# Top-32 attention with two expert layers: scores copied to SBUF by ScalarE, PSUM banks moved from scores to experts

## The chip, the core and the metric

One core of one Trainium2 chip runs the whole program. The metric is device time in microseconds of one execution. The kernel before was timed three times, and its median is 1330.06 us (1329.61 to 1332.45).

The engines are named as the profile names them: PE is TensorE's matmul side and PEld its weight loads, DVE is VectorE, ACT is ScalarE, POOL is GpSimd, and SP issues the DMAs. SBUF is the large on-chip memory, PSUM the small one (eight banks) that PE writes.

## The reference, cut to what matters

```python
# q, k, v: (4, 8, 576, 64)
scores = matmul(q, k^T) / 8
kth    = the 32nd largest score of each row
scores = where(scores >= kth, scores, -1e9)
attn   = exp(scores - rowmax);  attn /= attn.sum() + 1e-9
x      = matmul(attn, v)                       # -> (2304 tokens, 512)
h      = x @ w_in                              # 512 -> 2048
g      = where(h >= 1, h, where(h <= -1, 0, (h + 1)**2 / 4))
x      = g @ moe_w_out                         # 2048 -> 512
y      = silu(x @ w_gate) * (x @ w_val)        # 512 -> 1536
out    = y @ moe2_w_out                        # 1536 -> 512
```

All of it is in float32. The kernel gets there with TensorE's float32r format: nearly each operand is split into a high and a low part, and an expert product takes three passes.

## The kernel before, in words

The attention is worked in 32 units, a pair of heads by two or three query tiles of 128 rows. There are 144 score tiles of 128 queries by 576 keys. For each one PE writes scores into one of two PSUM tiles `pS` (two banks each), and DVE finds the 32nd largest value there: MAX8 (eight largest of a row, line 686) and MATCH_REPLACE8 (strike them out, line 696) take turns, the first of each reading `pS` and the later ones a copy `R` in SBUF that the first strike has written. ACT reads `pS` too and writes the exponentials into `E` (line 693). Last, DVE's mask (line 700, a scalar_tensor_tensor) compares `pS` with the 32nd value, multiplies with `E`, and sums the row. It holds `pS` until then, so PE's next score into this tile waits for it. The 576 entries of a row of `E` are then transposed on PE through two banks `pT`, moved out by ACT (lines 723 to 734), split on POOL (line 736), and multiplied with `v`.

The experts run between and behind, through two banks `pM`: first products on line 967, the second product of the first layer on 1009, that of the second layer on 1081. Their results are worked on by ACT and DVE (lines 1043 to 1115) and split by ACT and POOL (lines 873 and 875). All of the 68 weight slabs (512 KB) are split once on the chip, "converted" (lines 827 to 850): three operations on ACT, two on POOL, and on DVE one scalar_tensor_tensor (line 832), which reads one operand from `pM` in the first 24 slabs and both from SBUF in the other 44. The converted slab is stored to DRAM and loaded again for each step.

Nothing of the order is written by hand. A planner (`Plan`) gives each operation a cost by formulas, runs a list schedule forward and backward a few times over all engines and buffer rings, and emits the instructions of each engine in the order it finds. Each engine then executes its own queue in order, with semaphore waits. So a changed cost or ring size moves instructions on all engines.

Of the kernel before, what the change touches and what calls it, by code (L numbers as in the profile page):

```python
# [331 lines left out]
class Kernel:  # L332
# [53 lines left out]
    def dma(self, out, in_, nbytes, reads=(), writes=(), prio=5, tag="dma"):  # L386
        nc = self.nc
        self.p.op("DMA", nbytes / Plan.DMA_RATE, lambda: nc.sync.dma_start(out=out(), in_=in_()),
                  reads, writes, prio, tag, lat=Plan.DMA_LAT)


    def build(self):
# [9 lines left out]
        self.r_E = R("E", [128, 2, S], F32, 3)  # L402
# [118 lines left out]
    def prep_q(self, b, hp, qts):  # L521
# [80 lines left out]
    def outputs(self, b, hp, blk, V, PT, rs, rc):  # L602
# [7 lines left out]
        for h in (0, 1):  # L610
# [9 lines left out]
            p.op("ACT", self.act(N), lambda a=a, z=z, av=av: nc.scalar.activation(  # L620
# [33 lines left out]
    def qtile(self, t, i, qT, qz, kT, rs):  # L654
# [5 lines left out]
        for h in (0, 1) if t < 4 else (0,):  # L660
# [32 lines left out]
            p.op("ACT", self.act(576, self.FN - self.SB), lambda h=h, sc=sc, ee=ee: nc.scalar.activation(  # L693
                out=ee(), in_=sc(), func=AF.Exp, bias=nb[:, h:h + 1], scale=0.125), [ps, (nb, h)], [(Eb, h)], 1, "exp")
            for k in range(3):
                p.op("DVE", self.dve(576) + 0.06 + (0 if k else self.PS), lambda h=h, k=k, sc=sc, rr=rr: nc.vector.match_replace(  # L696
# [540 lines left out]
```

## Time and profile before

| what | value |
|---|---|
| timed runs, median (lowest to highest) | 1330.06 us (1329.61 to 1332.45) |
| profiled execution, span from first to last instruction | 1326.2 us |
| median less span (what lies around it) | 3.9 us |
| busy in the span: PE / DVE / ACT / POOL | 1208.5 / 1017.7 / 876.4 / 778.3 us |
| of the chain that ended last: PE / DMA / ACT / DVE / POOL | 68 / 9 / 7 / 7 / 6 % |
| matmuls | 7832 |

Busy time is the union of an engine's instructions. The profiled execution has no time of its own beside its span; the timed runs are other executions, and their median stands 3.9 us over it. The chain follows back from the last instruction to what released it, again and again. Shares over the whole span mix stages of different kind, so the rows further down are cut by stretches of time.

### The profile page before, as it was taken

To read this page: it belongs to the slowest core of one execution; us is meant where nothing else is said; L and a number is where in the kernel's file an instruction comes from. 1 tells how busy PE (TensorE), PEld (TensorE's weight loads), DVE (VectorE), ACT (ScalarE), POOL (GpSimd) and SP (SyncE) were. 2 spreads that over 40 slices of the span, in tenths; PEclk is the share of its full clock that TensorE was granted. 3 is DMA by queue.
4 is the path that set the end of the run, shared out by engine and by line. 5 is a ranking of instruction groups with operands and counts; after the bars stand their busy time and mean duration, and the time that the engine had idled before them with its cause. 6 is when DMAs were issued, how large, how long until landed. Compare 5 with 4: busy or idle time off the path is not lost.

```text
span 1326.2 us, 23321 instructions
## 1 busy us (share of the span) xinstructions
PE 1208.5 (91%) x7832; PEld 1095.6 (83%) x7832; DVE 1017.7 (77%) x2066; ACT 876.4 (66%) x1926; POOL 778.3 (59%) x831
## 2 busy tenths in 40 slices
PE   2556589888899999999999999999999999999998
PEld 2444489886799989998999988889999888888887
DVE  5899999899899989999999898989999312212212
ACT  6889799889777578776879777767766322333220
POOL 7888868689856465866667665556655313213210
PEclk9666699999899999999999999999999999999999
DMA  8788879789877786778676854548666754666452
GB/s 279 276 287 272 287 262 350 280 269 337 294 272 280 276 320 240 297 263 304 232 275 227 318 196 128 176 162 288 216 252 249 283 198 146 248 220 220 163 191 64
DMA packets 137032, 328.18 MB, mean 247 GB/s; under 512 B 21072, under 2 KB 66640, under 8 KB 136912
## 3 DMA queue, kind: packets, MB, share of 16 engines
q1 hardware_dynamic: 136912, 326.68, 70.2%
q8 instruction: 62, 1.02, 0.3%
q14 instruction: 58, 0.48, 0.1%
HBM read 282.07 MB, written 44.56 MB: 246 GB/s over the span
## 4 chain that ended last, share of the span: by engine, by line
PE 68%; DMA 9%; ACT 7%; DVE 7%; POOL 6%; issue 3%; SPq 0%; DVEq 0%; POOLq 0%; ACTq 0%
PE pM L967 25%; PE pM L1009 10%; PE pM L1081 7%; PE late L967 7%; PE pS L672 4%; PE pT L615 4%; PE late L1081 3%; PE pT L747 3%; DVE v L686 2%; PE late L1009 2%; DVE R L696 2%; POOL ct L835 2%; DMA cv<-in_moe_w_val_dram 2%; DMA cv<-in_moe_w_out_dram 1%; DMA w<-ws_moe_w_out 1%
## 5 line engine op out<-in xcount | busy, mean ns | idle before, releaser
L686 DVE MAX8 v<-R 128x8 f32<-128x576 f32 x432 | 315.1, 749 | 0.8
L967 PE MATMUL pM<-w,w 128*128 128x256 f32 (+1 forms) x1719 | 295.8, 319 | 3.5 <-DVE t L1105 2.5
L967 PEld LDWEIGHTS pM<-w,w 128*128 128x128 f32 x1719 | 249.9, 196 | 19.7 <-DVE t L1105 2.6
L736 POOL TENSOR_TENSOR PT<-F,PT 128x384 fp32r<-128x384 f32 (+2 forms) x192 | 176.7, 930 | 90.8 <-ACT F L734 84.4
L875 POOL TENSOR_TENSOR w<-t,w 128x512 fp32r<-128x512 f32 x110 | 142.2, 1295 | 135.1 <-ACT w L873 113.8
L696 DVE MATCH_REPLACE8 R<-v,R 128x576 f32<-128x576 f32 x288 | 213.8, 743 | 0.0
L686 DVE MAX8 v<-pS 128x8 f32<-128x576 f32 x144 | 109.3, 759 | 38.8 <-PE pS L672 36.3
L1009 PE MATMUL pM<-w,w 128*128 128x256 f32 (+1 forms) x867 | 132.2, 291 | 1.3 <-DVE t L1047 1.3
L693 ACT ACTIVATE E<-pS,nb 128x576 f32<-128x576 f32 x144 | 107.4, 746 | 25.3 <-DVE R L696 19.2
L747 PE MATMUL pT<-idf,E 128*128 128x128 f32 x512 | 95.9, 293 | 28.9 <-ACT qT L537 16.0
L1009 PEld LDWEIGHTS pM<-w,w 128*128 128x128 f32 x867 | 114.2, 190 | 4.0 <-DVE t L1047 2.7
L672 PE MATMUL pS<-kT,qT 128*128 128x288 f32 x512 | 100.9, 321 | 17.2 <-DVE E L700 14.9
L700 DVE SCALAR_TENSOR_TENSOR E<-pS,v,E 128x576 f32<-128x576 f32 x144 | 115.8, 804 | 0.2
L732 ACT ACTIVATE PT<-pT 128x384 fp32r<-128x384 f32 (+2 forms) x192 | 88.4, 463 | 40.6 <-PE pT L747 21.6
L696 DVE MATCH_REPLACE8 R<-v,pS 128x576 f32<-128x576 f32 x144 | 107.7, 748 | 0.0
L873 ACT ACTIVATE w<-t 128x512 fp32r<-128x512 f32 x110 | 70.5, 642 | 54.0 <-DVE t L1115 43.0
L835 POOL TENSOR_TENSOR ct<-ct,cv 128x512 int32<-128x512 int32 x68 | 91.4, 1348 | 22.9 <-ACT ct L830 15.1
L875 POOL TENSOR_TENSOR late<-t,late 128x512 fp32r<-128x512 f32 x32 | 41.3, 1293 | 103.8 <-ACT late L873 84.1
L747 PEld LDWEIGHTS pT<-idf,E 128*128 128x128 f32 x512 | 65.3, 148 | 42.6 <-ACT qT L537 18.1
L672 PEld LDWEIGHTS pS<-kT,qT 128*128 128x128 f32 x512 | 82.1, 206 | 22.3 <-DVE E L700 17.6
L967 PE MATMUL pM<-late,w 128*128 128x256 f32 (+1 forms) x597 | 98.5, 302 | 0.7 <-DVE t L1047 0.6
L615 PE MATMUL pT<-PT,v 128*128 128x256 f32 (+1 forms) x512 | 94.1, 310 | 3.9 <-ACT PT L727 3.1
(138 smaller groups left out, 2679.7 us busy)
## 6 DMA issues: line engine op xcount, KB each, us to landing
w<-ws_moe_w_out SPq DMA_DIRECT2D x134, 512.0 KB, 6.3
w<-ws_moe_w_in SPq DMA_DIRECT2D x90, 512.0 KB, 5.7
w<-ws_moe_w_val SPq DMA_DIRECT2D x55, 512.0 KB, 5.4
w<-ws_moe_w_gate SPq DMA_DIRECT2D x51, 512.0 KB, 6.3
late<-ws_moe_w_out SPq DMA_DIRECT2D x50, 512.0 KB, 5.3
cv<-in_moe_w_out_dram SPq DMA_DIRECT2D x28, 512.0 KB, 5.1
late<-ws_moe_w_in SPq DMA_DIRECT2D x28, 512.0 KB, 5.8
cv<-in_moe_w_in_dram SPq DMA_DIRECT2D x16, 512.0 KB, 5.0
```

Source lines behind the costliest of these rows:

```text
L615: nc.tensor.matmul(av[:, 0:N], V[:, h, c, :], PT[:, s, h * 4 + c, 0:N], start=s == 0 and c == 0, stop=False)
L672: nc.tensor.matmul(ps[:, j, 0:288], l(), kT[:, hh, at + j * 288:at + (j + 1) * 288], start=k == 0, stop=k == len(lhs) - 1)
L686: p.op("DVE", self.dve(576) + (0 if k else self.PS), lambda: nc.vector.max(out=v8[:, h, k, :], in_=rr() if k else sc()), [Rb if k else ps] ...
L696: p.op("DVE", self.dve(576) + 0.06 + (0 if k else self.PS), lambda h=h, k=k, sc=sc, rr=rr: nc.vector.match_replace(out=rr(), in_to_replace ...
L700: p.op("DVE", self.dve(576) + 0.06 + self.PS, lambda h=h, sc=sc, ee=ee: nc.vector.scalar_tensor_tensor(out=ee(), in0=sc(), scalar=v8[:, h, ...
L736: p.op("POOL", self.pool(n), lambda: nc.gpsimd.tensor_tensor(out=dst(1), in0=src(F), in1=dst(0).bitcast(F32), op=OP.subtract), [F, (PT, (0 ...
L747: fn = (lambda ps=ps, m=m, h=h, c=c: nc.tensor.transpose(ps[:, m * 128:(m + 1) * 128], Sb[:, h, 64 * h + c * 128:64 * h + (c + 1) * 128], ...
L835: p.op("POOL", self.pool(512), lambda: nc.gpsimd.tensor_tensor(out=ci(), in0=ci(), in1=word(0), op=OP.add), [(cv, 0)], [ct], 3, tag + "cvadd")
L875: p.op("POOL", self.pool(n), lambda: nc.gpsimd.tensor_tensor(out=dst[:, 1, to:to + n], in0=src[:, off:off + n], in1=dst[:, 0, to:to + n].b ...
L967: nc.tensor.matmul(ps[:, at:at + n], W[:, w, k * 128:(k + 1) * 128], x[:, s, xat:xat + n], start=k == 0 and j == 0, stop=k == KC - 1 and j ...
L1009: nc.tensor.matmul(ps[:, at:at + n], WO[f][:, v, j * 128:(j + 1) * 128], g[:, s, gat:gat + n], start=q == 0 and m == 0, stop=q == 3 and m ...
L1081: nc.tensor.matmul(ps[:], a[:, s, at:at + 128], WO[f][:, v, :], start=q == 0 and m == 0, stop=q == 3 and m == 2)
```

## The change

Each score tile is copied by ACT from PSUM into a new SBUF tile `C` (two of them), and the MAX8, the exponential, the first MATCH_REPLACE8 and the mask read `C`. With this `pS` is free once the copy is done. One `pS` tile (two banks) stays in place of two, and `pM` has four banks in place of two. `E` goes from three tiles to two. Some costs in the planner are raised: the DMA latency from 1.7 to 2.0 us, the loads of column-wise weight slabs, POOL's cost per element, two conversion operations on ACT, and ACT operations that move data between partition halves. The extra cost that the planner put on DVE operations for reading PSUM is gone from the score tile's operations, since they read SBUF now.

```diff
 class Plan:
-    DMA_LAT = 1.7
+    DMA_LAT = 2.0
...
     SB, FN, PS, PORT = 0.043, 0.136, 0.065, 0.0
+    CVX, XP = 0.045, 0.125
...
-        return 0.149 + n * 0.0021
+        return 0.149 + n * 0.00215
...
-        self.p.op("DMA", nbytes / Plan.DMA_RATE, lambda: nc.sync.dma_start(out=out(), in_=in_()),
+        rate = 310e3 if tag.endswith("ldw64") and narrow else Plan.DMA_RATE
+        self.p.op("DMA", nbytes / rate, lambda: nc.sync.dma_start(out=out(), in_=in_()),
...
-        self.r_E = R("E", [128, 2, S], F32, 3)
+        self.r_E = R("E", [128, 2, S], F32, 2)
...
-        self.p_s = R("pS", [128, 2, 512], F32, 2, "P")
+        self.p_s = R("pS", [128, 2, 512], F32, 1, "P")
+        self.r_C = R("C", [128, S], F32, 2)
-        self.p_m = R("pM", [128, 512], F32, 4 - self.PT_BANKS, "P")
+        self.p_m = R("pM", [128, 512], F32, 6 - self.PT_BANKS, "P")
...
-            def vmax(k, h=h, ps=ps, Rb=Rb, sc=sc, rr=rr):
-                p.op("DVE", self.dve(576) + (0 if k else self.PS), lambda: nc.vector.max(
-                    out=v8[:, h, k, :], in_=rr() if k else sc()), [Rb if k else ps], [(v8, (h, k))], 6, "max8")
+            Cb = self.r_C.new()
+
+            def cc(Cb=Cb):
+                return Cb[:].rearrange("p (j n) -> p j n", j=2)
+            p.op("ACT", self.act(576), lambda sc=sc, cc=cc: nc.scalar.activation(out=cc(), in_=sc(), func=AF.Copy), [ps], [Cb], 1, "scp")
+            def vmax(k, h=h, Cb=Cb, Rb=Rb, cc=cc, rr=rr):
+                p.op("DVE", self.dve(576), lambda: nc.vector.max(
+                    out=v8[:, h, k, :], in_=rr() if k else cc()), [Rb if k else Cb], [(v8, (h, k))], 6, "max8")
...
-            p.op("ACT", self.act(576, self.FN - self.SB), lambda h=h, sc=sc, ee=ee: nc.scalar.activation(
-                out=ee(), in_=sc(), func=AF.Exp, bias=nb[:, h:h + 1], scale=0.125), [ps, (nb, h)], [(Eb, h)], 1, "exp")
+            p.op("ACT", self.act(576, self.FN), lambda h=h, cc=cc, ee=ee: nc.scalar.activation(
+                out=ee(), in_=cc(), func=AF.Exp, bias=nb[:, h:h + 1], scale=0.125), [Cb, (nb, h)], [(Eb, h)], 1, "exp")
...
-            p.op("DVE", self.dve(576) + 0.06 + self.PS, lambda h=h, sc=sc, ee=ee: nc.vector.scalar_tensor_tensor(
-                out=ee(), in0=sc(), scalar=v8[:, h, 3, 7:8], in1=ee(),
+            p.op("DVE", self.dve(576) + 0.06, lambda h=h, cc=cc, ee=ee: nc.vector.scalar_tensor_tensor(
+                out=ee(), in0=cc(), scalar=v8[:, h, 3, 7:8], in1=ee(),
                 op0=OP.is_ge, op1=OP.mult, accum_out=rs[:, i, h:h + 1]),
-                [ps, (v8, (h, 3))], [(Eb, h), (rs, (i, h))], 5, "mask")
+                [Cb, (v8, (h, 3))], [(Eb, h), (rs, (i, h))], 5, "mask")
...
-        p.op("ACT", self.act(512, self.SB), lambda: nc.scalar.activation(
+        p.op("ACT", self.act(512, self.SB + self.CVX), lambda: nc.scalar.activation(
             out=bits(), in_=cv[:].bitcast(U16).rearrange("p (n t) -> p n t", t=4)[:, :, 1], func=AF.Copy,
```

The changed program has 144 instructions more, all on ACT; the count of every other instruction is the same. Three places show what moves. In these rows a name is a tile with its buffer number, and lines of the changed kernel are 3 to 8 higher (mask 700 is 708, exponential 693 is 701, copy 692, score 672 is 675).

On DVE, near the 60th score tile, before (masks on line 700 read `pS`):

```order
L700 SCALAR_TENSOR_TENSOR E_199,rs_210<-pS_250,v_204,E_199 128x576
L696 MATCH_REPLACE R_200<-v_204,R_200 128x576
L686 MAX v_204<-R_200 128x8
L696 MATCH_REPLACE R_200<-v_204,R_200 128x576
L686 MAX v_202<-pS_250 128x8
```

The same place in the changed kernel (the mask is on line 708):

```order
L708 SCALAR_TENSOR_TENSOR E_197,rs_209<-C_250,v_203,E_197 128x576
L694 MAX v_203<-R_199 128x8
L704 MATCH_REPLACE R_199<-v_203,R_199 128x576
L694 MAX v_203<-R_199 128x8
L694 MAX v_201<-C_250 128x8
```

In both, three instructions of the other tile stand between a mask and the next MAX8 that reads the same buffer. Before, PE's score has to be made in this gap; now ACT's copy has to be.

On PE, about the same place, before, with the waits (`pS1` is a score tile, `pM` an expert bank):

```order
L747 MATMUL pT0_251<-idf_160,E0_197 128x128 [waits Activation_49]
L672 MATMUL pS1_250<-kT0_193,qT0_191 128x288 [waits DVE_49]
L672 MATMUL pS1_250<-kT0_193,qT0_191 128x288 x3
L747 MATMUL pT0_251<-idf_160,E0_197 128x128 x2
L747 MATMUL pT1_252<-idf_160,E0_197 128x128 [waits Activation_49]
```

And in the changed kernel:

```order
L975 MATMUL pM3_256<-w4_224,w2_222 128x256 [waits DMAHW1_49]
L975 MATMUL pM3_256<-w4_224,w2_222 128x256 x5
L675 MATMUL pS0_248<-kT0_193,qT0_191 128x288 [waits Activation_49]
L675 MATMUL pS0_248<-kT0_193,qT0_191 128x288 x3
L975 MATMUL pM3_256<-w0_220,w2_222 128x256 x6
```

A score's wait for DVE's mask has become a wait for ACT's copy, and expert products now use banks up to `pM3`. Counted over the whole order, 239,616 columns of expert products stood ahead of PE's 201st score matmul (of 640) before, and 254,208 do now; ahead of the 161st it was 168,960 and is 179,712.

On ACT of the changed kernel, about the same place (the copies are on line 692; before, a row like them stood nowhere):

```order
L692 ACTIVATE C_249<-pS_248 128x576
L623 ACTIVATE tmp_217<-pT_252 64x320
L540 ACTIVATE qT_191<-pT_252 128x2x256
L626 ACTIVATE y_218<-pT_251 64x320
L701 ACTIVATE E_197<-C_249,nb_204 128x576
L540 ACTIVATE qT_191<-pT_252 64x2x256
L881 ACTIVATE w_231<-t_240 128x512
L540 ACTIVATE qT_191<-pT_252 64x2x256
L895 ACTIVATE t_237<-pM_253 128x512
L692 ACTIVATE C_250<-pS_248 128x576
```

What stood behind the exponential alone now stands behind a copy as well: moves out of `pT`, splits and expert results. A copy waits for PE's score and for DVE's mask of the tile two before, whose `C` it takes.

## Rows read from the trace of the kernel before

**Rows 1.** The page: span, and busy tenths of each engine in 40 slices.

```profile
span 1326.2 us, 23321 instructions
...
PE   2556589888899999999999999999999999999998
DVE  5899999899899989999999898989999312212212
ACT  6889799889777578776879777767766322333220
POOL 7888868689856465866667665556655313213210
```

**Rows 2.** Busy time by stretch (columns in the first line of the view).

```profile
core 0: us, PE busy (x) PEld busy (x) DVE busy (x) ACT busy (x) POOL busy (x), PEclk, DMA share, GB/s
0.00:100.00 100.00, 46.65 (x196) 36.63 (x196) 76.68 (x158) 80.51 (x165) 79.20 (x83) 0.75 0.82 281
100.00:200.00 100.00, 69.19 (x396) 58.71 (x397) 94.08 (x183) 88.73 (x191) 78.71 (x76) 0.76 0.79 274
200.00:300.00 100.00, 91.57 (x701) 88.73 (x700) 95.85 (x190) 85.20 (x188) 80.20 (x77) 0.97 0.86 300
300.00:400.00 100.00, 87.37 (x617) 79.80 (x616) 91.52 (x189) 82.35 (x182) 80.07 (x83) 0.97 0.85 299
...
900.00:1000.00 100.00, 97.28 (x783) 94.93 (x782) 97.05 (x205) 74.46 (x160) 57.64 (x73) 1.00 0.71 254
1000.00:1100.00 100.00, 100.00 (x593) 89.11 (x592) 45.85 (x89) 37.38 (x77) 32.81 (x35) 1.00 0.68 246
...
```

**Rows 3.** The same view, in three long stretches (same columns).

```profile
0.00:400.00 400.00, 294.77 (x1906) 263.87 (x1907) 358.13 (x717) 336.79 (x723) 318.19 (x317) 0.86 0.83 289
400.00:1040.00 640.00, 631.73 (x4676) 598.24 (x4675) 596.29 (x1258) 467.33 (x1082) 395.74 (x463) 1.00 0.71 251
1040.00:1326.00 286.00, 281.99 (x1254) 233.48 (x1252) 63.32 (x92) 72.25 (x122) 64.35 (x52) 1.00 0.53 183
```

**Rows 4.** DVE's groups of the whole span: busy us, mean ns, idle before.

```profile
L686 DVE MAX8 v<-R 128x8 f32<-128x576 f32 x432 | 315.1, 749 | 0.8
L686 DVE MAX8 v<-pS 128x8 f32<-128x576 f32 x144 | 109.3, 759 | 38.8 <-PE pS L672 36.3 <-PE pT L747 1.4 <-PE pT L544 0.5
L696 DVE MATCH_REPLACE8 R<-v,R 128x576 f32<-128x576 f32 x288 | 213.8, 743 | 0.0
L696 DVE MATCH_REPLACE8 R<-v,pS 128x576 f32<-128x576 f32 x144 | 107.7, 748 | 0.0
L832 DVE SCALAR_TENSOR_TENSOR cv<-cv 128x512 int32<-128x512 int32 x44 | 43.1, 980 | 4.5 <-ACT cv L827 3.0 <-issue 1.4
L832 DVE SCALAR_TENSOR_TENSOR cv<-cv,pM 128x512 int32<-128x512 int32 x24 | 16.5, 685 | 22.0 <-ACT pM L827 21.1 <-issue 0.9
```

**Rows 5.** Line 832: each operand pair's shortest, median and longest ns.

```profile
engine op xcount: duration ns min/median/max, first and last start us, forms
...
L832 DVE SCALAR_TENSOR_TENSOR cv<-cv x44: 669/822/1798, 102.1 to 319.3; 128x512 int32<-128x512 int32 x44
L832 DVE SCALAR_TENSOR_TENSOR cv<-cv,pM x24: 671/688/697, 7.1 to 95.4; 128x512 int32<-128x512 int32 x24
```

**Rows 6.** DVE in order of time: start us, us.

```profile
283.94 1.80 DVE L832 SCALAR_TENSOR_TENSOR cv<-cv 128x512 int32<-128x512 int32 x1
285.66 0.08 DVE L696 MATCH_VALUE_LOAD R<-v,R 128x8 f32 x1
285.73 0.74 DVE L696 MATCH_REPLACE8 R<-v,R 128x576 f32<-128x576 f32 x1
```

**Rows 7.** POOL in the same stretch.

```profile
283.87 1.32 POOL L875 TENSOR_TENSOR w<-t,w 128x512 fp32r<-128x512 f32 x1
285.12 1.80 POOL L835 TENSOR_TENSOR ct<-ct,cv 128x512 int32<-128x512 int32 x1
```

**Rows 8.** DVE's mask group from 0 to 400 us.

```profile
L700 DVE SCALAR_TENSOR_TENSOR E<-pS,v,E 128x576 f32<-128x576 f32 x49 | 39.4, 804 | 0.2
```

**Rows 9.** DVE's mask group from 400 to 1040 us.

```profile
L700 DVE SCALAR_TENSOR_TENSOR E<-pS,v,E 128x576 f32<-128x576 f32 x95 | 76.4, 805 | 0.0
```

**Rows 10.** ACT's groups of the whole span.

```profile
L693 ACT ACTIVATE E<-pS,nb 128x576 f32<-128x576 f32 x144 | 107.4, 746 | 25.3 <-DVE R L696 19.2 <-POOL nb L690 3.0 <-POOL PT L736 1.7
L501 ACT ACTIVATE kT<-pT 128x512 fp32r<-128x512 f32 x32 | 19.1, 596 | 4.5 <-PE pT L498 4.2
L883 ACT ACTIVATE big<-pM 128x512 f32<-128x512 f32 x30 | 18.1, 602 | 17.7 <-PE pM L1081 13.9 <-PE pM L1009 3.7
L873 ACT ACTIVATE w<-t 128x512 fp32r<-128x512 f32 x110 | 70.5, 642 | 54.0 <-DVE t L1115 43.0 <-DMA t<-xs 6.3 <-PE late L1081 2.7
```

**Rows 11.** POOL's groups of the whole span.

```profile
L736 POOL TENSOR_TENSOR PT<-F,PT 128x384 fp32r<-128x384 f32 x144 | 145.5, 1019 | 79.3 <-ACT F L734 75.1 <-PE pS L672 3.6 <-DMA w<-ws_moe_w_out 0.3
L875 POOL TENSOR_TENSOR w<-t,w 128x512 fp32r<-128x512 f32 x110 | 142.2, 1295 | 135.1 <-ACT w L873 113.8 <-PE pM L1009 11.8 <-issue 6.2
L835 POOL TENSOR_TENSOR ct<-ct,cv 128x512 int32<-128x512 int32 x68 | 91.4, 1348 | 22.9 <-ACT ct L830 15.1 <-DVE cv L832 3.0 <-DMA cv<-in_moe_w_val_dram 1.6
```

**Rows 12.** Waits from 0 to 400 us: total us, times, longest.

```profile
PE pS L672 <- DVE E L700: 14.1, 9, 5.8
DVE v L686 <- PE pS L672: 5.9, 9, 1.8
```

**Rows 13.** Waits from 400 to 1040 us.

```profile
DVE v L686 <- PE pS L672: 30.4, 48, 1.6
```

**Rows 14.** The chain that ended last: one piece in order of time.

```profile
1042.61 27.90 PE pM L967 x123
```

More of the change, by code (lines that the diff above doesn't have):

```diff
@@ L384, in mm, with dma @@
         return k * (0.0133 + n / 2400.0)
-    def dma(self, out, in_, nbytes, reads=(), writes=(), prio=5, tag="dma"):
+    def dma(self, out, in_, nbytes, reads=(), writes=(), prio=5, tag="dma", narrow=False):
         nc = self.nc
-        self.p.op("DMA", nbytes / Plan.DMA_RATE, lambda: nc.sync.dma_start(out=out(), in_=in_()),
+        rate = 310e3 if tag.endswith("ldw64") and narrow else Plan.DMA_RATE
+        self.p.op("DMA", nbytes / rate, lambda: nc.sync.dma_start(out=out(), in_=in_()),
                   reads, writes, prio, tag, lat=Plan.DMA_LAT)
@@ L536, in prep_q @@
             for i, (dst, src, s) in enumerate((self.SAME, *self.SWAP)):
-                p.op("ACT", self.act(512), lambda dst=dst, src=src, s=s, ps=ps: nc.scalar.activation(
+                p.op("ACT", self.act(512, self.XP * (i > 0)), lambda dst=dst, src=src, s=s, ps=ps: nc.scalar.activation(
                     out=qT[dst, :, s, :], in_=ps[src].rearrange("p (h n) -> p h n", h=2), func=AF.Copy), [ps], [(qT, i)], 2, "qTe")
@@ L548, in prep_q @@
                 for i, (dst, src, s) in enumerate((self.SAME, *self.SWAP)):
-                    p.op("ACT", self.act(64), lambda h=h, dst=dst, src=src, s=s, ps=ps: nc.scalar.activation(
+                    p.op("ACT", self.act(64, self.XP * (i > 0)), lambda h=h, dst=dst, src=src, s=s, ps=ps: nc.scalar.activation(
                         out=qz[dst, h, s, h * 64:h * 64 + 64], in_=ps[src, h * 192:h * 192 + 64], func=AF.Copy), [ps], [(qz, (h, i))], 2, "qTe")
@@ L596, in spread @@
             for h in (0, 1):
-                p.op("ACT", self.act(64), lambda h=h: nc.scalar.activation(
+                p.op("ACT", self.act(64, self.XP), lambda h=h: nc.scalar.activation(
                     out=rb[64 * h:64 * h + 64, w:w + 64], in_=psr[64 * h:64 * h + 64, w + 64 * h:w + 64 + 64 * h], func=AF.Copy, scale=2.0),
@@ L619, in outputs @@
             a, z = 64 * h, 64 - 64 * h
-            p.op("ACT", self.act(N), lambda a=a, z=z, av=av: nc.scalar.activation(
+            p.op("ACT", self.act(N, self.XP), lambda a=a, z=z, av=av: nc.scalar.activation(
                 out=tmp[a:a + 64, 0:N], in_=av[z:z + 64, 0:N], func=AF.Copy), [av], [(tmp, h)], 2, "ave")
@@ L692, in qtile @@
                 [(v8, (h, 0))], [(nb, h)], 2, "nb")
[L693 to L694 removed]
+            p.op("ACT", self.act(576, self.FN), lambda h=h, cc=cc, ee=ee: nc.scalar.activation(
+                out=ee(), in_=cc(), func=AF.Exp, bias=nb[:, h:h + 1], scale=0.125), [Cb, (nb, h)], [(Eb, h)], 1, "exp")
             for k in range(3):
[L696 to L698 removed]
+                p.op("DVE", self.dve(576) + 0.06, lambda h=h, k=k, cc=cc, rr=rr: nc.vector.match_replace(
+                    out=rr(), in_to_replace=v8[:, h, k, :], in_values=rr() if k else cc(), imm_value=NEG),
+                    ([] if k else [Cb]) + [(v8, (h, k))], [Rb], 6, "mrep")
                 vmax(k + 1)
[L700 to L701 removed]
+            p.op("DVE", self.dve(576) + 0.06, lambda h=h, cc=cc, ee=ee: nc.vector.scalar_tensor_tensor(
+                out=ee(), in0=cc(), scalar=v8[:, h, 3, 7:8], in1=ee(),
                 op0=OP.is_ge, op1=OP.mult, accum_out=rs[:, i, h:h + 1]),
[L703 removed]
+                [Cb, (v8, (h, 3))], [(Eb, h), (rs, (i, h))], 5, "mask")
         return Eb
@@ L826, in bits @@
             return low[:].bitcast(I32) if bank else word(0)
-        p.op("ACT", self.act(512, self.SB), lambda: nc.scalar.activation(
+        p.op("ACT", self.act(512, self.SB + self.CVX), lambda: nc.scalar.activation(
             out=bits(), in_=cv[:].bitcast(U16).rearrange("p (n t) -> p n t", t=4)[:, :, 1], func=AF.Copy,
             scale=2.0 ** -13, bias=2.0 ** -14 - 0.5), [(cv, 0)] if bank else [], [(low, 0)], 3, tag + "cvl")
-        p.op("ACT", self.act(512, self.SB), lambda: nc.scalar.activation(
+        p.op("ACT", self.act(512, self.SB + self.CVX), lambda: nc.scalar.activation(
             out=ct[:], in_=word(1, F32), func=AF.Sign), [(cv, 1)], [ct], 3, tag + "cvs")
```

6 lines of the change are left out of this document (2 added, 4 removed).

## Prediction, made before the changed kernel was run

> **What bounds the kernel now.** I read the page's tenths first [rows 1]. PE is below 9 tenths in most of the first ten slices (about 330 us) and at 9 nearly throughout from then on. DVE is at 8 or 9 until about 1040 us and at 1 to 3 after. So there are three stretches, and the busy times give each its limit [rows 2, 3].
>
> From 0 to 400 us PE is busy 294.8 of 400 us: 105 us of PE's idle time lie here, against 8 us from 400 to 1040 and 4 us after. DVE is at 358, ACT at 337, POOL at 318. Here attention and the conversion of the weights run at the pace of DVE, ACT and POOL together, and PE has too few expert products that may start. From 400 to 1040 us PE is busy 631.7 of 640 and DVE 596.3: PE sets the pace, with DVE close behind it. From 1040 us on there are no score tiles, and PE works alone (282 of 286 us).
>
> It follows that whatever delays attention in the first stretch delays the end one for one, because PE has no reserve later to make it good. In the second stretch DVE may become slower by what is idle in it, some 44 us, but PE executes in order, so a late mask also stops expert products behind a transpose that waits for it.
>
> **The change part by part.**
>
> *DVE's reads.* Reading the copy in place of PSUM takes 749 ns against 759 for a MAX8 and 743 against 748 for a MATCH_REPLACE8 [rows 4]. The shortest of line 832 with both operands in SBUF is 669 ns, against a median of 688 with one in PSUM [rows 5], so an undisturbed mask should take 19 ns less than its 804 [rows 8]. These savings are 10 + 5 + 19 = 34 ns a tile, 4.9 us for 144.
>
> *The mask's second operand.* This is the term that decides. The mask now reads two operands in SBUF (`C` and `E`). The kernel has one DVE operation of this kind already: line 832 takes 685 ns with one operand in PSUM and 980 ns with both in SBUF, 0.31 us more than the undisturbed 669, with single ones up to 1798 [rows 4, 5]. The order of time shows why: at 283.94 us one starts 0.07 us after POOL's line 875, whose 1.32 us end at 285.19; 0.55 us later the DVE instruction is done, after 1.80 us, and the POOL instruction that started at 285.12 is held up in its turn, 1.80 us against a mean of 1.35 [rows 6, 7, 11]. So each waits until the other's instruction ends.
>
> [...]
>
> By the row a mask waits 0.31 us where POOL is busy 318 of 400 us; in the second stretch POOL is busy 396 of 640 [rows 3], so I scale to 0.31 x 0.618 / 0.795 = 0.24 us. There are 49 masks in the first stretch and 95 in the second [rows 8, 9]. DVE's work grows by 49 x 0.31 = 15.2 less the savings of 49 x 0.034 = 1.7, that is 13.5 us, and by 95 x (0.24 - 0.034) = 19.6 us in the second. The bounds are nothing (every mask falls between POOL's instructions) and the longest row's 1.80 - 0.67 = 1.13 us for each mask, 55 us in the first stretch. I take the mean, since 44 instructions in the midst of the same POOL work made it.
>
> *What covers it.* The score matmul no longer waits for the mask, and three score tiles may stand ready (two `C` and `pS`) where two could. DVE waited 5.9 us for scores in the first stretch and 30.4 in the second [rows 12, 13]. In the first I take these 5.9 as gained back: 13.5 - 5.9 = +7.6 us at the end. In the second PE sets the pace, and 19.6 us fit into the 30.4 if they come at the right moments. I charge a quarter, +5 us, since PE's queue waits in order for masks that come later than the planner thinks: its cost of a mask fell from 0.794 to 0.729, while I expect it to rise from 0.80 to about 1.03.
>
> *The copies on ACT.* A copy of 128x576 out of PSUM is not in the trace; 128x512 take 596 to 602 ns, and the exponential of 128x576 takes 746 [rows 10]. By length the copy is 602 x 576 / 512 = 0.68 us. The exponential from SBUF costs perhaps 40 ns more (642 against 602 for 128x512) [rows 10]. That is 144 x 0.72 = 104 us on ACT, 35 of them in the first stretch, where ACT would go from 337 to 372 of 400 us. The idle 28 us cover it on paper; if that cover were gone, as much as the whole 35 would show. Behind a copy stand moves out of `pT`, for which PE waits, and conversion steps, for which POOL waits. I take +3 us, a tenth, with 0 and 35 as ends.
>
> *Banks, E and order.* Four `pM` banks let the planner put expert products earlier: 14,592 columns more stand ahead of the 201st score matmul. The chain has 123 products of 512 columns in 27.9 us, 0.227 us each [rows 14], so 14,592 columns are 28.5 such products, or 6.5 us of PE's work that moves into the stretch where PE idles. I count -6.5 us. Its ends are 0, if the products don't find their weights there, and twice that, 13. `E` with two tiles in place of three makes an exponential wait until the transposes of the tile pair two before are done. I price it at nothing: a score tile takes DVE about 6 us (four MAX8, three MATCH_REPLACE8 and the mask [rows 4, 8]), and this work hides the transposes. Should it not, the exponentials come late by what the transposes lack, and the masks behind them with it. The planner's other raised costs change no duration, only the order.
>
> **The sum.** +7.6 + 5 + 3 - 6.5 = +9.1 us on the span of 1326.2, so 1335.3; with the 3.9 us that the median of the runs stands above this span it is 1339 us.
>
> **Rivals.** A measurement of this kernel can tell about 0.2% (2.7 us) from no change.
>
> *The deeper score buffer wins (faster).* PE stood 14.1 us for a mask to free `pS` in the first stretch [rows 12], in nine waits of up to 5.8 us, and these stop the transposes and moves queued behind. If they vanish and DVE's own waits take up the masks' wait (5.9 us, and the rest lies in DVE's 42 us of idle time there), the end comes 14.1 + 6.5 - 3 = 17.6 us sooner: 1312 us. It decides as soon as the mask's wait is below about 0.1 us a tile in the first stretch. For it speaks that PE's idle time is all there; against it that DVE idles only 18.6 us from 100 to 400 us [rows 2], of which the masks' wait would take 13.5. Half of it would be 1321. Chance 0.30. [...]
>
> *The waits fit (no change).* DVE's idle time takes up the port's wait in both stretches, ACT's takes the copies, and the products moved ahead find no idle PE: 1330 us, chance 0.12.
>
> *ACT becomes the limit (slower still).* A copy waits at the head of ACT's queue for the mask of two tiles before, and everything behind it waits too. Then the first stretch grows by ACT's 35 us and half of the other terms: about 1370 us. For it speaks ACT's 93%; against it that the planner knows of the copies. Chance 0.08.
>
> **Chances and range.** The forecast, a wait of masks for POOL that is partly covered, has 0.50, and with it all outcomes from 1333 to 1355. Slower has 0.50 + 0.08 = 0.58, the same 0.12, faster 0.30. The range reaches into the faster rival's 1316 and up to 1358, leaving 0.1 on either side. The likeliest case's own range is 1333 to 1355.
>
> **What would show it.** The mask's group should have a mean of 1.0 to 1.1 us with a longest near 1.8, while MAX8 and MATCH_REPLACE8 stay within 15 ns of before. PE should no longer wait for DVE's mask at scores, but for ACT's copy. ACT's busy time should be near 980 us. PE's idle time up to 400 us should grow from 105 to about 110, and from 400 to 1040 from 8 to about 13 or more. If masks stay near 0.8 us, the step on the port is wrong, and the time should be at or below 1322. If masks are slow and the time still falls, the cover was larger than I think: PE's idle time in the first stretch would then be well below 100 us.

## The result, and the profile after

The changed kernel took 1313.99 us (median of four runs, 1311.37 to 1317.29) against 1331.26 for the kernel before on the same chip. The ratio is 0.988, with a 95% interval of 0.9856 to 0.9904: 16 to 17 us faster, where I had forecast 9 us slower. The profiled execution is the longest of the four: 1317.29 us with a span of 1315.5, 10.7 us below the span of before. The comparison of traces explains these 10.7 us.

The page's busy times and tenths of the changed kernel:

```profile
span 1315.5 us, 23512 instructions
...
PE 1209.5 (92%) x7832; PEld 1097.6 (83%) x7832; DVE 1052.7 (80%) x2066; ACT 951.0 (72%) x2070; POOL 830.4 (63%) x831
...
PE   2566687897999999999999999999999999999998
DVE  5998998999999999999999999999999512222212
ACT  7898999998998689777989887879877421333220
POOL 6886888899878566866677875567754512213210
```
DVE has a 9 in all but a few of the slices up to 1030 us, more than before [rows 1]. Busy time in the three stretches (the last is 275 us long now):

```profile
0.00:400.00 400.00, 299.76 (x1907) 266.66 (x1908) 366.90 (x693) 357.37 (x760) 335.88 (x311) 0.91 0.85 292
400.00:1040.00 640.00, 638.35 (x4723) 606.38 (x4723) 625.27 (x1286) 525.06 (x1195) 433.16 (x473) 1.00 0.71 253
1040.00:1315.00 275.00, 271.35 (x1205) 224.59 (x1203) 60.53 (x88) 68.60 (x117) 61.31 (x49) 1.00 0.51 179
```
PE's busy time over the span is the same as before, 1209.5 us against 1208.5 (the page gives both). So the gain is PE's idle time: 117.7 us of the span before, 106.0 now. Up to 400 us it fell from 105 to 100 us, and from 400 to 1040 us from 8.3 to 1.7 us, though DVE works 28.9 us more in this second stretch [rows 3]. What is left of both after 1040 us is PE's work alone, 282 us before and 271 now. In both kernels the last mask starts at 1033 us (1032.8 and 1033.3, in the rows of masks below): attention was not faster, but PE had done more of the experts by its end. The order says how much: ahead of the last score matmul, which starts at 1023 us in both, stand 2376 expert products (counted as products of 512 columns, of 3672 in all) before and 2422.5 now. The 46.5 are 10.6 us at 0.227 us each [rows 14], and that is the whole gain of this execution.

DVE's groups of the changed kernel; the mask's durations (shortest, median, longest ns; first and last start), before and then in the changed kernel; and POOL's groups of the changed kernel:

```profile
L694 DVE MAX8 v<-R 128x8 f32<-128x576 f32 x432 | 314.5, 746 | 1.2
L708 DVE SCALAR_TENSOR_TENSOR E<-C,v,E 128x576 f32<-128x576 f32 x144 | 154.4, 1073 | 1.2 <-ACT E L701 1.1
L694 DVE MAX8 v<-C 128x8 f32<-128x576 f32 x144 | 107.7, 748 | 14.6 <-ACT C L692 11.9 <-ACT rs L717 1.4 <-POOL PT L744 0.5
L704 DVE MATCH_REPLACE8 R<-v,C 128x576 f32<-128x576 f32 x144 | 106.6, 740 | 0.0
L840 DVE SCALAR_TENSOR_TENSOR cv<-cv 128x512 int32<-128x512 int32 x44 | 45.6, 1038 | 5.7 <-ACT cv L835 3.7 <-ACT PT L740 0.7 <-POOL hq L487 0.5
```
```profile
L700 DVE SCALAR_TENSOR_TENSOR E<-pS,v,E x144: 790/804/818, 30.9 to 1032.8; 128x576 f32<-128x576 f32 x144
```
```profile
L708 DVE SCALAR_TENSOR_TENSOR E<-C,v,E x144: 792/972/1906, 30.1 to 1033.3; 128x576 f32<-128x576 f32 x144
```
```profile
L744 POOL TENSOR_TENSOR PT<-F,PT 128x384 fp32r<-128x384 f32 x144 | 152.9, 1072 | 53.1 <-ACT F L742 47.8 <-DMA w<-ws_moe_w_val 2.5 <-PE pS L675 2.2
L883 POOL TENSOR_TENSOR w<-t,w 128x512 fp32r<-128x512 f32 x111 | 147.6, 1332 | 173.5 <-ACT w L881 143.6 <-issue 13.8 <-PE late L1017 11.8
L843 POOL TENSOR_TENSOR ct<-ct,cv 128x512 int32<-128x512 int32 x68 | 94.9, 1398 | 15.0 <-DVE cv L840 5.2 <-ACT ct L838 2.8 <-ACT C L692 2.5
```
The mask went from 804 to 1073 ns, with single ones up to 1906; MAX8 and MATCH_REPLACE8 from the copy take 748 and 740 ns, as little less as the rows said [rows 4]. POOL's instructions are longer in turn: line 736 (744 now) takes 1072 ns against 1019 before, line 835 (843 now) 1398 against 1348 [rows 11]. DVE's busy time rose from 1017.7 to 1052.7 us. So the mask's wait for POOL, which the prediction also calls the port's, is there, in the size forecast.

ACT's two groups of the score tile, and the waits around it, from 0 to 400 us and from 400 to 1040 us:

```profile
L701 ACT ACTIVATE E<-C,nb 128x576 f32<-128x576 f32 x144 | 113.2, 786 | 11.4 <-POOL nb L698 10.8
L692 ACT ACTIVATE C<-pS 128x576 f32<-128x576 f32 x144 | 94.4, 655 | 20.7 <-DVE E L708 17.5 <-PE pS L675 2.1
```
```profile
PE pS L675 <- ACT C L692: 20.5, 16, 2.6
ACT C L692 <- DVE E L708: 6.3, 8, 1.2
DVE v L694 <- ACT C L692: 6.1, 8, 1.4
```
```profile
ACT C L692 <- DVE E L708: 11.3, 12, 3.0
DVE v L694 <- ACT C L692: 5.7, 9, 1.2
```
PE's wait of 14.1 us for masks up to 400 us [rows 12] has not gone away. It is 20.5 us for ACT's copies now. DVE's waits for scores, 5.9 and 30.4 us [rows 12, 13], are waits for copies of 6.1 and 5.7 us.

### The profile page after: what moved, and what is told of

The parts are those of the page before. It is cut to its first block, busy times and chain, and to the rows that moved or that the text cites. A ratio compares the mean times of both kernels' runs of the same rounds, so it can differ in the third digit from the quotient of the medians.

```text
span 1315.5 us, 23512 instructions
## 1 busy us (share of the span) xinstructions
PE 1209.5 (92%) x7832; PEld 1097.6 (83%) x7832; DVE 1052.7 (80%) x2066; ACT 951.0 (72%) x2070; POOL 830.4 (63%) x831
## 3 DMA queue, kind: packets, MB, share of 16 engines
q8 instruction: 62, 1.02, 0.3%
## 4 chain that ended last, share of the span: by engine, by line
PE 70%; DMA 8%; POOL 8%; ACT 6%; DVE 4%; issue 3%; SPq 1%; POOLq 0%; ACTq 0%; DVEq 0%
PE pM L975 28%; PE pM L1017 10%; PE pM L1089 8%; PE late L975 5%; PE pS L675 4%; PE pT L618 4%; PE late L1017 3%; PE pT L755 3%; PE late L1089 2%; POOL ct L843 2%; DMA cv<-in_moe_w_out_dram 1%; POOL PT L744 1%; DMA cv<-in_moe_w_gate_dram 1%; DMA ws_moe_w_gate<-cv 1%; POOL cv L858 1%
## 5 line engine op out<-in xcount | busy, mean ns | idle before, releaser
L975 PE MATMUL pM<-w,w 128*128 128x256 f32 (+1 forms) x2019 | 341.5, 313 | 4.1 <-POOL w L858 3.0
L975 PEld LDWEIGHTS pM<-w,w 128*128 128x128 f32 x2019 | 285.9, 192 | 22.0 <-POOL w L858 4.1
L883 POOL TENSOR_TENSOR w<-t,w 128x512 fp32r<-128x512 f32 x111 | 147.6, 1332 | 173.5 <-ACT w L881 143.6
L744 POOL TENSOR_TENSOR PT<-F,PT 128x384 fp32r<-128x384 f32 (+2 forms) x192 | 190.2, 1001 | 59.0 <-ACT F L742 52.5
L708 DVE SCALAR_TENSOR_TENSOR E<-C,v,E 128x576 f32<-128x576 f32 x144 | 154.4, 1073 | 1.2 <-ACT E L701 1.1
L1017 PE MATMUL pM<-w,w 128*128 128x256 f32 (+1 forms) x828 | 124.6, 289 | 1.1 <-POOL w L858 1.1
L701 ACT ACTIVATE E<-C,nb 128x576 f32<-128x576 f32 x144 | 113.2, 786 | 11.4 <-POOL nb L698 10.8
L694 DVE MAX8 v<-C 128x8 f32<-128x576 f32 x144 | 107.7, 748 | 14.6 <-ACT C L692 11.9
L1017 PEld LDWEIGHTS pM<-w,w 128*128 128x128 f32 x828 | 109.5, 191 | 2.0 <-POOL w L858 1.5
L692 ACT ACTIVATE C<-pS 128x576 f32<-128x576 f32 x144 | 94.4, 655 | 20.7 <-DVE E L708 17.5
L755 PE MATMUL pT<-idf,E 128*128 128x128 f32 x512 | 94.9, 292 | 13.9 <-ACT PT L735 4.0
L704 DVE MATCH_REPLACE8 R<-v,C 128x576 f32<-128x576 f32 x144 | 106.6, 740 | 0.0
L843 POOL TENSOR_TENSOR ct<-ct,cv 128x512 int32<-128x512 int32 x68 | 94.9, 1398 | 15.0 <-DVE cv L840 5.2
L742 ACT ACTIVATE F<-pT 128x384 f32<-128x384 f32 (+2 forms) x192 | 89.2, 470 | 6.6 <-POOL PT L744 6.0
L975 PE MATMUL pM<-w,late 128*128 128x256 f32 (+1 forms) x486 | 87.9, 319 | 0.1
```

Source lines behind the costliest of these rows:

```text
L694: p.op("DVE", self.dve(576), lambda: nc.vector.max(out=v8[:, h, k, :], in_=rr() if k else cc()), [Rb if k else Cb], [(v8, (h, k))], 6, "max8")
L704: p.op("DVE", self.dve(576) + 0.06, lambda h=h, k=k, cc=cc, rr=rr: nc.vector.match_replace(out=rr(), in_to_replace=v8[:, h, k, :], in_valu ...
L708: p.op("DVE", self.dve(576) + 0.06, lambda h=h, cc=cc, ee=ee: nc.vector.scalar_tensor_tensor(out=ee(), in0=cc(), scalar=v8[:, h, 3, 7:8], ...
L744: p.op("POOL", self.pool(n), lambda: nc.gpsimd.tensor_tensor(out=dst(1), in0=src(F), in1=dst(0).bitcast(F32), op=OP.subtract), [F, (PT, (0 ...
L755: fn = (lambda ps=ps, m=m, h=h, c=c: nc.tensor.transpose(ps[:, m * 128:(m + 1) * 128], Sb[:, h, 64 * h + c * 128:64 * h + (c + 1) * 128], ...
L843: p.op("POOL", self.pool(512), lambda: nc.gpsimd.tensor_tensor(out=ci(), in0=ci(), in1=word(0), op=OP.add), [(cv, 0)], [ct], 3, tag + "cvadd")
```

## The experiments

I set three theories against each other. *Copy*: more score tiles stand ready, and this makes the gain (the rival of my prediction that came nearest in time). *Banks*: four `pM` banks do. *Order*: the raised planner costs do, through the order alone. Times are medians; each chip's time of the kernel before, 1329 to 1331 us, is the comparison.

**The raised costs alone, in the kernel before.** All cost edits of the change's diff, none of the others.

```diff
-    DMA_LAT = 1.7
+    DMA_LAT = 2.0
+    CVX, XP = 0.045, 0.125
-        return 0.149 + n * 0.0021
+        return 0.149 + n * 0.00215
...
```

> The kernel before with the planner's raised costs alone (no copy, banks and E as before), so nothing changes but the order. If truer costs in the order make the gain (theory Order), about 1314 us, with PE idle near 100 us up to the last mask. If the copies or the banks make it (theories Copy and Banks), 1327 to 1334 us, PE idle near 113 us up to the last mask.

1320.4 us, ratio 0.9928 (0.9900 to 0.9957): 10 us faster, by the order alone. One execution of it, the first two stretches:

```profile
0.00:400.00 400.00, 303.56 (x1973) 273.19 (x1974) 366.50 (x732) 344.30 (x741) 325.32 (x323) 0.89 0.84 293
400.00:1040.00 640.00, 632.91 (x4659) 600.01 (x4658) 590.17 (x1245) 461.65 (x1074) 395.22 (x462) 1.00 0.69 250
```
PE's idle time up to 400 us is 96.4 us, less than in the changed kernel, and from 400 to 1040 us it is 7.1. The gain comes another way than in the change: ahead of the last score matmul stand 2376 products, as in the kernel before, but it starts 9 us sooner (1014.1 against 1023.0).

**The changed kernel with the old costs.**

```diff
-    DMA_LAT = 2.0
+    DMA_LAT = 1.7
-    CVX, XP = 0.045, 0.125
-        return 0.149 + n * 0.00215
+        return 0.149 + n * 0.0021
...
```

> The changed kernel with the old planner costs: copies, one pS tile, four pM banks, two E tiles. Theories Copy and Banks: 1312 to 1318 us. Theory Order: 1330 us or, with the masks' wait for POOL uncovered, up to 1339.

1332.1 us, ratio 1.0020 (1.0006 to 1.0035). Copies and banks without the costs gain nothing. The last score matmul has 2412 products ahead of it, nearly as many as in the changed kernel, but starts 14 us later (1036.9 against 1023.3). Theory Copy falls as the sole cause, and so does Banks.

**The changed kernel with the banks as before.**

```diff
-        self.p_s = R("pS", [128, 2, 512], F32, 1, "P")
+        self.p_s = R("pS", [128, 2, 512], F32, 2, "P")
-        self.p_m = R("pM", [128, 512], F32, 6 - self.PT_BANKS, "P")
+        self.p_m = R("pM", [128, 512], F32, 4 - self.PT_BANKS, "P")
...
```

> The changed kernel with the banks as before (two pS tiles, two pM banks); copies and raised costs stay. Theory Copy (scores are free early and more tiles stand ready): 1310 to 1317 us, for pS has even one tile more. Theory Banks (four pM banks let expert products start earlier): 1326 to 1335 us. The masks take 1.05 to 1.1 us in either.

1347.8 us, ratio 1.0133 (1.0101 to 1.0164). Against the costs alone, the copy, the masks on SBUF and two tiles of `E` in place of three lose 27 us together (no run parts them), and moving two banks from `pS` to `pM` gives 34 us back. Two stretches of this run, the second from its last mask to its end; the last stretch of the changed kernel, from its last mask; and the masks of this run:

```profile
0.00:400.00 400.00, 294.78 (x1794) 259.77 (x1795) 374.38 (x686) 355.06 (x748) 329.34 (x306) 0.82 0.81 277
1035.00:1348.80 313.80, 308.39 (x1460) 259.21 (x1459) 69.58 (x103) 78.64 (x137) 70.76 (x58) 1.00 0.57 204
```
```profile
1034.00:1315.50 281.50, 277.35 (x1237) 229.66 (x1235) 62.45 (x93) 72.86 (x126) 65.33 (x52) 1.00 0.51 178
```
```profile
L708 DVE SCALAR_TENSOR_TENSOR E<-C,v,E 128x576 f32<-128x576 f32 x144 | 169.3, 1176 | 0.7 <-ACT E L701 0.3
```
PE has 308.4 us of work left behind the last mask against 277.4. The order says the same: ahead of the 601st score matmul stand 2088 expert products with two banks and 2214 with four, and both start it at 956 us. The 126 that lie behind are 28.6 us at 0.227 us each [rows 14]. Not all of the 34 us need be the banks', for in the changed kernel's order a mask takes 1073 ns and not 1176, which is 15 us of DVE's work.

**Two banks, and the mask reads PSUM again.** As the run before, but `pS` is held until the mask.

```diff
-                out=ee(), in0=cc(), scalar=v8[:, h, 3, 7:8], in1=ee(),
+                out=ee(), in0=sc(), scalar=v8[:, h, 3, 7:8], in1=ee(),
```

> As the run with banks as before, but the mask alone reads pS again (it holds pS until then, and its planned cost is the old one), while MAX8, MATCH_REPLACE8 and the exponential read the copy. The mask should fall from about 1.07 to 0.80 us, and DVE's busy time by 35 to 40 us. If the wait for POOL is hidden wholly in DVE's idle time: the same time as with the mask on the copy, within 4 us. If it costs what I predicted (7 to 13 us): that much faster, unless pS held longer brings back the waits for scores (20 us or more between PE and DVE).

1339.1 us, ratio 1.0072 (1.0046 to 1.0099): 9 us faster than with the mask on the copy. The mask takes 804 ns again, and DVE's busy time falls from 1069.3 to 1025.2 us, but MAX8's idle time before it rises from 12.6 to 48.1 us, since `pS` is held longer. So this run does not give the price of the wait for POOL alone; a later one does.

**The changed kernel in a slightly other order.** The planner's general latency at 0.53 in place of 0.52.

```diff
-    LAT = .52
+    LAT = .53
```

> The changed kernel with the planner's general latency at 0.53 in place of 0.52 us: the same program but for a slightly other order. It measures how much of a difference is the luck of one order. If the gains of the cost edits are steady: 1311 to 1317 us. If an order's time scatters by as much as the cost edits seemed to give (10 to 18 us), it may lie anywhere from 1305 to 1332.

1318.2 us, ratio 0.9918 (0.9903 to 0.9933). This one other order is 4 to 5 us slower. It is a single sample of an order's luck, and the next run shows a larger step.

**The changed kernel, with a planner that knows what the mask takes**, and what a conversion with both operands in SBUF takes.

```diff
-    SB, FN, PS, PORT = 0.043, 0.136, 0.065, 0.0
+    SB, FN, PS, PORT = 0.043, 0.136, 0.065, 0.35
...
-            p.op("DVE", self.dve(576) + 0.06, lambda h=h, cc=cc, ee=ee: nc.vector.scalar_tensor_tensor(
+            p.op("DVE", self.dve(576) + 0.33, lambda h=h, cc=cc, ee=ee: nc.vector.scalar_tensor_tensor(
```

> The changed kernel, where the planner is told what the masks and the 44 conversions with both operands in SBUF take (0.27 us more for a mask, 0.35 for a conversion); no instruction changes but its place. If truer costs make better orders in general (theory Order): 1303 to 1311 us. If only the costs of the change did, or the masks' wait is hidden in DVE's idle time anyway: 1311 to 1318 us.

1332.2 us, ratio 1.0022 (1.0009 to 1.0036): 18 us worse than the changed kernel, outside both ranges. Truer costs do not make better orders in general, and these 18 us are a change of order alone. The masks of this run (shortest, median, longest; first and last start):

```profile
L708 DVE SCALAR_TENSOR_TENSOR E<-C,v,E x144: 790/892/1909, 28.7 to 1063.6; 128x576 f32<-128x576 f32 x144
```
Its last mask starts 30 us later than in the changed kernel. In this order 63 conversions stand ahead of the 33rd mask in place of 56, and 2262 products ahead of the 601st score matmul in place of 2214. PE is busy for 1215.7 us, with more idle time than in the changed kernel.

**Three `pM` banks.**

```diff
-        self.p_m = R("pM", [128, 512], F32, 6 - self.PT_BANKS, "P")
+        self.p_m = R("pM", [128, 512], F32, 5 - self.PT_BANKS, "P")
```

> The changed kernel with three pM banks in place of four (one PSUM bank lies unused); one pS tile as in the change. With two pS tiles and two pM banks it was 1348 us. If the number of pM banks makes that difference: between 1318 and 1335 us. If it came from the second pS tile's side of that run (order, not banks): 1311 to 1317 us.

1333.3 us, ratio 1.0022 (1.0012 to 1.0033). With two, three and four banks, all with the raised costs, the times are 1347.8, 1333.3 and 1314.0 us (the run with two has a second `pS` tile). Here too the banks are not the only thing that differs: the masks of the order with three banks take 1218 ns (shown further down), 21 us of DVE's work more than those with four. And with four banks the change takes from 1314 to 1332 us, by its costs.

**One `pS` tile and four `pM` banks without the copy**, with the raised costs.

```diff
-        self.p_s = R("pS", [128, 2, 512], F32, 2, "P")
+        self.p_s = R("pS", [128, 2, 512], F32, 1, "P")
-        self.p_m = R("pM", [128, 512], F32, 4 - self.PT_BANKS, "P")
+        self.p_m = R("pM", [128, 512], F32, 6 - self.PT_BANKS, "P")
...
```

> One pS tile and four pM banks and the raised costs, without the copy: DVE and the exponential read pS as before, three E tiles. With one pS tile PE's next score can start only when a tile's mask is done, so DVE has nothing of the next tile to fill its waits with. Theory Copy (the copy is what makes the bank move possible): DVE idles a microsecond or more per tile, 144 us or more in all, and the time is 1400 us or above. Theory Banks alone: 1300 to 1320 us, as the copy's and the port's costs are gone.

1752.9 us, ratio 1.3184 (1.3164 to 1.3203). The copy's worth is that it makes the bank move possible.

**The masks' wait for POOL taken away.** Three `pM` banks as above, in the same order of instructions, but the mask multiplies with ones from the unused PSUM bank.

```diff
+        self.flat_one = pools["P"].tile([128, 512], F32, name="flat_one")
+        nc.vector.memset(self.flat_one, 1.0)
...
-                out=ee(), in0=cc(), scalar=v8[:, h, 3, 7:8], in1=ee(),
+                out=ee(), in0=cc(), scalar=v8[:, h, 3, 7:8], in1=self.flat_one[:, None, 0:288].to_broadcast([128, 2, 288]),
```

> As the run with three pM banks, in the same order of instructions, but the mask's second operand is a PSUM bank of ones in place of E in SBUF (the bank that lies unused there), so the mask has one operand in SBUF. It leaves out the multiplication with the exponential. The mask should fall from about 1.1 to 0.80 us, its longest to 0.85 and DVE's busy time by 40 us. If the masks' wait for POOL is hidden by DVE's idle time: 1333 us as with three banks, within 3. If it delays the end as I predicted (about 12 us of the 33): 1318 to 1325 us. If DVE sets the pace wherever it is over 97% busy, more than half of the 40 us comes back: 1313 us or less.

1309.0 us, ratio 0.9852 (0.9823 to 0.9881): 23 to 24 us faster than with three banks. The mask's group and the first two stretches of the run with three banks, then the same of this one:

```profile
L708 DVE SCALAR_TENSOR_TENSOR E<-C,v,E 128x576 f32<-128x576 f32 x144 | 175.3, 1218 | 2.7 <-ACT E L701 2.2
```
```profile
0.00:400.00 400.00, 303.98 (x1885) 265.28 (x1886) 371.86 (x687) 356.35 (x756) 330.91 (x308) 0.87 0.83 288
400.00:1040.00 640.00, 629.13 (x4663) 595.43 (x4663) 631.11 (x1280) 521.13 (x1184) 424.83 (x467) 1.00 0.69 248
```
```profile
L708 DVE SCALAR_TENSOR_TENSOR E<-C,v,flat_one 128x576 f32<-128x576 f32 x144 | 115.6, 803 | 2.5 <-ACT E L701 1.8
```
```profile
0.00:400.00 400.00, 308.42 (x1954) 273.15 (x1955) 361.58 (x709) 362.05 (x772) 321.12 (x318) 0.88 0.85 296
400.00:1040.00 640.00, 637.94 (x4705) 605.24 (x4704) 600.13 (x1272) 520.74 (x1188) 400.83 (x468) 1.00 0.70 250
```
The mask falls from 1218 to 803 ns, DVE's busy time over the span by 49 us (1070.9 to 1021.6; 41 of them up to 1040 us), and POOL's by 45 us (826.5 to 781.3). PE's idle time up to 1040 us falls by 13 us (96.0 + 10.9 against 91.6 + 2.1) and its busy time over the span by 8 (1220.9 to 1213.0), and so 21 us less of PE's work lie behind 1040 us. About half of DVE's extra work reached the end. I had no way to keep the multiplication without `E` in SBUF, as all eight banks are taken in the change, so this is no version of the kernel.

**What of the costs it is.** First the DMA costs alone in the kernel before.

```diff
-    DMA_LAT = 1.7
+    DMA_LAT = 2.0
...
+        rate = 310e3 if tag.endswith("ldw64") and narrow else Plan.DMA_RATE
```

> The kernel before with the raised DMA costs alone (latency 2.0 us and the slower column-wise loads). With all raised costs it took 1320 us. If the DMA's part of the costs made that gain: 1317 to 1323 us. If ACT's and POOL's part did: 1328 to 1333 us.

1328.8 us, ratio 1.0003 (0.9988 to 1.0018): nothing. The kernel before with the latency of 0.53 us alone:

```diff
-    LAT = .52
+    LAT = .53
```

> The kernel before with the planner's latency at 0.53 in place of 0.52 us, another measure of the luck of an order. If one order is like another within 4 us, as for the changed kernel: 1326 to 1334 us. If the gain of the cost edits in the kernel before (10 us) is within that scatter: anywhere from 1315 to 1340 us.

1329.2 us, ratio 0.9996 (0.9979 to 1.0013): an order like the old one. The engine costs alone, in the kernel before:

```diff
+    CVX, XP = 0.045, 0.125
-        return 0.149 + n * 0.0021
+        return 0.149 + n * 0.00215
...
```

> The kernel before with the raised engine costs alone (ACT's moves between partition halves, two conversion operations, POOL per element), DMA costs as before. The DMA costs alone gave 1329 us, all together 1320. If the engine costs make the gain: 1317 to 1323 us. If it takes both together, or it is luck of an order: 1326 to 1333 us.

1326.5 us, ratio 0.9972 (0.9958 to 0.9986): 4 us of the 10. All costs in the kernel before with the latency of 0.53 us:

```diff
-    LAT = .52
+    LAT = .53
```

> The kernel before with all raised costs, and the planner's latency at 0.53 in place of 0.52 us. Without the latency it took 1320 us. If the gain of the costs is steady: 1316 to 1325 us. If it was the luck of one order: 1326 us or more.

1324.3 us, ratio 0.9956 (0.9941 to 0.9972): 6 us in place of 10. In the changed kernel, with the DMA costs taken back:

```diff
-    DMA_LAT = 2.0
+    DMA_LAT = 1.7
...
+        rate = Plan.DMA_RATE
```

> The changed kernel with the raised engine costs and the old DMA costs. If the engine costs make the gain of 18 us: 1312 to 1319 us. If the DMA costs do: 1328 to 1334 us. Between these: each has a part.

1322.9 us, ratio 0.9949 (0.9935 to 0.9964). And with the engine costs taken back:

```diff
-    CVX, XP = 0.045, 0.125
+    CVX, XP = 0.0, 0.0
-        return 0.149 + n * 0.00215
+        return 0.149 + n * 0.0021
```

> The changed kernel with the raised DMA costs and the old engine costs. If the DMA costs make the gain here: 1312 to 1319 us. If the engine costs do: 1328 to 1334 us.

1324.2 us, ratio 0.9961 (0.9944 to 0.9978). Taking back either half of the costs loses about half of the 18 us.

**A planner that thinks masks faster still.**

```diff
-            p.op("DVE", self.dve(576) + 0.06, lambda h=h, cc=cc, ee=ee: nc.vector.scalar_tensor_tensor(
+            p.op("DVE", self.dve(576) - 0.14, lambda h=h, cc=cc, ee=ee: nc.vector.scalar_tensor_tensor(
```

> The changed kernel with the planner told that a mask takes 0.53 us, 0.2 less than now, while it takes 1.07. Told more (0.27 us more, and 0.35 more for conversions) the time rose by 18 us. If a plan that thinks DVE faster than it is keeps scores ahead of expert products and so gains: 1304 to 1312 us. If each departure from the costs of the change only loses or scatters: 1314 to 1330 us.

1329.6 us, ratio 1.0009 (0.9994 to 1.0024). Neither a truer nor a rosier cost of the mask helps. No version was faster than the changed kernel but the one that leaves out the multiplication with `E`.

**All orders side by side.** The changed kernel's instructions ran in seven orders: 1314.0, 1318.2, 1322.9, 1324.2, 1329.6, 1332.1 and 1332.2 us. Those of the kernel before ran in six: 1320.4, 1324.3, 1326.5, 1328.8, 1329.2 and about 1330. These orders are no fair sample, but their ranges overlap, so the difference of 17 us is not one of instructions alone. Two numbers of each order tell most of its time: how many products stand ahead of the last (640th) score matmul, and when that matmul starts. One profiled execution each:

| order | products ahead | start, us | span, us |
|---|---|---|---|
| kernel before | 2376 | 1023.0 | 1326.2 |
| the same, raised costs | 2376 | 1014.1 | 1317.1 |
| change, old costs | 2412 | 1036.9 | 1331.5 |
| change | 2422.5 | 1023.3 | 1315.5 |
| change, two banks | 2256 | 1012.7 | 1348.8 |
| change, three banks | 2383.5 | 1028.8 | 1331.9 |
| three banks, mask without `E` | 2383.5 | 1007.6 | 1310.8 |

The start plus 0.227 us for each product that is left of the 3672 lies 9 to 15 us below the span in all seven.

## Why the prediction was wrong

*The step that failed* is the sentence "The planner's other raised costs change no duration, only the order", which priced them at nothing. They are worth -10 us in the kernel before and -18 us in the change. With the old costs the forecast nearly holds: the last score matmul starts 13.9 us later than in the kernel before, where I had +15.6 (7.6, 5 and 3), and 36 products more stand ahead of it, 8.2 us, where I had -6.5. The median is 1332.1 us, slower if only just (+1.5 us; the profiled spans differ by 5.3). The raised costs then bring that matmul 13.6 us forward and put 10.5 more products, 2.4 us, ahead of it: 16 us, the whole way from one span to the other. I had expected PE's idle time up to 400 us to grow from 105 to about 110 us, with no term that could shrink it; the costs alone take it to 96.

*The wait for POOL.* Right in mechanism and in size on DVE: 1073 ns against the 1.0 to 1.1 us forecast, DVE's work +35.0 us against +33.1 net. In the changed kernel's trace the 42 masks that start with POOL idle take 792 to 816 ns. The 102 that start within a POOL instruction take 1184 ns in the mean, and the 85 of them over 850 ns end 0.61 to 0.62 us after it. POOL waits in its turn: the 16 instructions of 128x384 on line 744 that start within a mask take 1.53 us in the median, the others 1.02. In the kernel before, with `pS` in PSUM, masks take 805 ns within a POOL instruction and 804 outside. The size hangs on the order too: with two and with three banks the mask's mean is 1176 and 1218 ns. With one operand in PSUM it takes 803 ns in the same order as those 1218. Of the cover, I took 12.6 of 33.1 us (7.6 and 5) to reach the end, 0.38 of them; taking the wait away gave 24 of 49.3 us of DVE's work with three banks, 0.49, with POOL's relief in it. At that share 33.1 us would be 16 (an estimate), so this term was some 3 us too small and did not turn the sign. With four banks it could not be tried.

*Reads.* MAX8 and MATCH_REPLACE8 are right: 748 and 740 ns from the copy, against 759 and 748. The 19 ns of the mask are not there: its shortest is 792 ns now and 790 before. I had set the shortest of one group of line 832 against the median of the other. Between PSUM and the copy a MAX8 saves 11 ns here and a MATCH_REPLACE8 8.

*ACT.* The copy takes 655 ns (0.68 forecast) and the exponential 786, 40 ns more, as forecast. The durations of ACT's instructions add up to 102 us more, near the 104 forecast, but they overlap in the trace, so ACT's busy time is 951 us, not 980. The +3 us for its queue were not tried by themselves.

*Banks and E.* Against the kernel before, to which my -6.5 us belongs, the count by the last score matmul gives -8.2 us with the old costs and -10.6 with the raised ones: the right way, somewhat small. Against the same kernel on two banks the banks are worth -34 us (-19 for the fourth alone), with the raised costs and with what the masks' waits differ in these orders. I had not asked that question: without the banks the copy leaves 120 products fewer ahead of the last score matmul than the kernel before (2256 against 2376), though that matmul starts 10 us sooner. `E` with two tiles was not varied by itself. In the changed kernel ACT's idle time before exponentials is 11.4 us, 10.8 of it for POOL's `nb`, so a wait for transposes to free `E` does not show; what it does to the order is not known.

*The way from 1330 to 1314*, in one order of steps: the costs, -10; copies, masks on SBUF and two tiles of `E` with two banks, +27; two more banks, -34. Other orders of the steps give other parts: with the old costs, copies and banks together give +1.5.

*The rival that gave 1312* had the time for another reason than it gave. It had PE's waits at scores vanish; they are 20.5 us, longer than before. What it had right was that DVE's idle time takes up much of the masks' work: up to 1040 us DVE idled for 85.6 us before and 47.8 now.

*What stays open.* Why these costs give a better order. It is no matter of truth alone, as the true cost of a mask made it worse by 18 us. A latency of 0.53 us in place of 0.52 moved the time by 0 to 5 us in three orders, so the part of 4 to 10 us of each half is near that, while another planned cost of the mask, with all raised costs in place (in one of the two runs with another cost of the conversions too), lost 16 to 18 us. That the change's costs were a fortunate point among orders I can argue, as each of six departures from them lost 4 to 18 us, but it is not shown.

## What to carry to other kernels

Where a planner writes the order, take a fixed point in it and ask two things: how much of the bound engine's work stands ahead of it, and when it is reached. The count alone misleads: two orders of the same instructions with 2376 products ahead differ by 9 us. A cost table that changes no instruction is an edit like any other, and here it decided the sign; try it alone first, and try the change in more than one order before calling its time the change's. Beside a busy POOL (830 of 1315 us here) the mask with both tiles in SBUF cost far more than its undisturbed row: 1073 to 1218 ns in the mean of three orders, 792 at its shortest, 803 to 804 in the mean with one operand in PSUM. So in a kernel like this keep one operand of such an instruction in PSUM if a bank can be spared, and weigh that bank against what else it could hold.

## What was unexpected of the hardware

The granted clock differed between the orders. In the traces of both kernels it stands at 0.5 or at 1.0 of full speed and changes between them 22 times in the first 360 us before and 18 times in the first 332 us of the changed kernel; the mean up to 400 us was 0.91 of full speed in the changed kernel and 0.82 with two banks, for the same matmuls in all. Over the whole span four executions of each gave 0.965 to 0.974 and 0.942 to 0.962. One order's executions differ as well, though: 20 of the kernel before on one chip had 0.952 to 0.970, so a single profile shows little of this. PE's busy time over the span was 1209.5 and 1225.6 us in these two profiles: of the 33 us between their spans, 16 are PE's busy time and not waits, and they are part of the 34 us that the two banks gave.
